# A new order of the pieces in a fused attention and max-out kernel, with a ones product for one more half and whole-tensor packing copies

## The chip, the cores and the metric

The kernel runs on one core of a Trainium2 chip. The metric is the device time of one execution in microseconds (us). Engines named below: PE multiplies matrices into PSUM (PEld loads its weights), DVE and ACT work on vectors and read PSUM, POOL works on SBUF alone and also issues the loads that cast fp32 to bf16, SP issues the stores.

## The reference

Eight batches, eight heads, 576 positions, head size 64, 32 memory slots. An attention over compressed keys and values is followed by a feed-forward layer whose hidden value is the maximum of three products:

```python
a = softmax(phi)                                  # over the 32 slots, per position
k_m = einsum('bhsm,bhsd->bhmd', a, k)             # 32 compressed keys per head
v_m = einsum('bhsm,bhsd->bhmd', a, v)
attn = softmax(q @ k_m.T / 8)                     # over the 32 slots
x = (attn @ v_m), heads side by side              # 4608 x 512
h = max(x @ w1, x @ w2, x @ w3)                   # 4608 x 768
out = h @ w_out                                   # 4608 x 512, fp32
```

## The kernel before

Two identities carry the work. First, the product with v_m is folded into the weights: for each batch, `fold` multiplies v_m into w1 - w3 and w2 - w3, so that the feed-forward reads the attention directly. Second, max(a, b, c) = max(a - c, b - c, 0) + c, so the third product is not formed for every hidden column; w3 times w_out is computed once (`w3_t`, `w3_o`, the tile `w3o`), folded per batch (`wp3`), and added in the last product.

The program is a long list of pieces. Each piece is a word such as `F8@3`: a letter and a number for the kind, and the batch after the @. A sign ! at the end swaps which of ACT and DVE copies the result out of PSUM. The list at the end of the function is written out in full, and every engine runs its share of the pieces in exactly this order; an engine that waits holds up everything behind it on the same engine. The kinds:

- H, L, Y (POOL): loads. H loads a half of k or v of batch 0, L0 phi, L1 k, L2 v, L3 q; Y0 to Y2 load w1 to w3 and Y3 loads w_out. The phi of batch 0 comes from SP. All POOL loads go through one software queue.
- I (POOL): the identity matrix for transposes, and the column of ones in two packed tiles `kvr`.
- r0, r1 (POOL): from batch 2 on, copies k (r0) or v (r1) into `kvr`, where k, v and a one stand side by side for each position.
- E (ACT): exp of phi. B (PE): the compressed keys and values, 72 small products. N (DVE): their division by the sum. K (PE, then DVE or ACT): their transpose. For batches 0 and 1, B, N and K come in two parts, 0 for k and 1 for v.
- Q0, Q1 (DVE): transposes of q. S (PE, then two exps on ACT): scores; it takes two PSUM tiles.
- The second softmax's division, in one of two ways for each batch and half g. The usual one: a (DVE transpose), s (DVE sum), c (DVE reciprocal), m (POOL product), X (DVE transpose back). For the pairs in the set `ONES`: M (PE, a product with a block matrix of ones gives the sums in every row), R (ACT: Ln, then Exp of its negative), X (DVE product).
- D0 to D3 (PE, then a copy to SBUF): fold; D3 makes `wp3`. V (DVE): the differences w1 - w3, w2 - w3, in place.
- F0 to F11 (PE): the feed-forward's first product, one hidden tile each; even ones are copied with relu to `h`, odd ones end in a DVE maximum that writes `hT`. T0 to T4 (PE, ACT copy, SP store): the second product for 128 rows. The last T3 is done in two halves.
- W, O: the one-time product of w3 and w_out. Z: warm-up products that nobody reads.

All PSUM tiles come from one pool of four; a piece that needs a tile waits for the copy out of the tile four places before it. The software DMA queue has eight places for loads in flight, so a load also waits for the landing of the eighth before it. `kvo`, `kvr`, `qT`, `e`, `wp` and others have two buffers.

Lines to follow: `pack` 103, `load_kv` 96, `ones_sum` 326, `ones_rec` 340, `ones_mul` 352, `att_t` 361, `att_mul` 383, `att_back` 393, `fold` 401, `ffn1` 433, `ffn2` 465, the set `ONES` 205, the list 571 to 594.

Of the kernel before, what the change touches and what calls it, by code (L numbers as in the profile page):

```python
# [15 lines left out]
def kernel(  # L16
# [12 lines left out]
    nc = tc.nc  # L29

    B, H, S, D = q.shape
    M = phi.shape[-1]
    P = 128
    NP = H // 2
# [28 lines left out]
    kvos = []  # L63
    for i in range(2):
        kvo = const.tile([P, 3, NP, NC, D], BF16, name=f"kvo{i}")
        kvos.append(kvo)
    kvrs = [
        const.tile([P, NP, NC, 2 * D + 2], BF16, name=f"kvr{i}") for i in range(2)
    ]
# [31 lines left out]
        )  # L101

    def pack(b, i):
        for j in range(NP):
            nc.gpsimd.tensor_copy(  # L105
                out=kvrs[b % 2][:, j, :, D * i : D * (i + 1)], in_=kvos[b % 2][:, i, j]
            )

    def load_q(b):
        qq = inp.tile([P, NP, NC, D], BF16, name="qq")  # L110
# [91 lines left out]
            c = e  # L202

    ln = const.tile([P, S], FP32, name="ln")
    ONES = {(0, 0), (0, 1)}
    st = {}

    def att_exp(b, js=slice(0, NP)):
# [117 lines left out]
    def ones_sum(b, g):  # L326
        s = st[b]
        e2 = s["e2"]
        sm = acc_pool.tile([P, 2, BANK], FP32, name="sm", tag="acc")
        for h in range(2):  # L330
            nc.tensor.matmul(
                sm[:, h, 0:SH],
                lhsT=blkones,
                rhs=e2[:, g, h * SH : (h + 1) * SH],
                start=True,
                stop=True,
            )
        s["sm", g] = sm
# [44 lines left out]
    def att_mul(b, g):  # L383
        s = st[b]
        t = s["t", g]
        nc.gpsimd.tensor_tensor(  # L386
            out=t,
            in0=t,
            in1=s["sm", g].unsqueeze(2).to_broadcast([P, S // HP, R, 2]),
            op=ALU.mult,  # L390
        )
# [146 lines left out]
    def issue(b, n, swap):  # L538

        i = int(n[1:]) if len(n) > 1 else None  # L540
        {
            "I": lambda: [make_identity(nc, ident)]
            + [nc.gpsimd.memset(x[:, :, :, 2 * D : 2 * D + 1], 1.0) for x in kvrs],
            "Y": lambda: load_w(i) if i < 3 else load_wo(),
            "L": lambda: load_ph(b) if i == 0 else load_q(b) if i == 3 else load_kv(b, i - 1),
            "H": lambda: load_kv(b, i % 2, halves[i // 2]),
            "r": lambda: pack(b, i),
            "E": lambda: [att_exp(b, h) for h in (halves if b == 0 else [slice(0, NP)])],
            "B": lambda: att_kv(b, i),
            "N": lambda: att_kv_norm(b, i),  # L550
            "K": lambda: att_kv_t(b, swap, i),
            "Q": lambda: att_q(b, i),
            "S": lambda: att_score(b),
            "a": lambda: att_t(b, i),
            "s": lambda: att_sum(b, i),
            "c": lambda: att_rec(b, i),
            "m": lambda: att_mul(b, i),
            "X": lambda: (ones_mul if (b, i) in ONES else att_back)(b, i),
            "M": lambda: ones_sum(b, i),
            "R": lambda: ones_rec(b, i),  # L560
            "D": lambda: fold(b, i, swap),
            "F": lambda: ffn1(b, i, swap),
            "T": lambda: ffn2(b, i, swap),
            "W": lambda: w3_t(i, swap),
            "O": lambda: w3_o(i, swap),
            "V": lambda: w_diff(i),
            "Z": lambda: warm_up(i),
        }[n[0]]()


    for w in """
        H0@0 H2@0 I@0 L3@0 Y2@0 E@0 Y3@0 Z25@0 B0@0 H3@0 N0@0 Z2@0 K0@0! H1@0 Q1@0 Q0@0 Z9@0
        S@0 Z2@0 M0@0 R0@0 W2@0 M1@0 Y0@0 W0@0 Y1@0 L0@1 R1@0 X1@0 L1@1 X0@0 W1@0! Z7@0 O0@0
        O2@0 O3@0 B1@0 N1@0 O1@0 K1@0 L3@1 D3@0 D1@0 D0@0 F8@0 V0@0 F10@0 F0@0 F6@0! F2@0 L2@1
        D2@0 L1@2 V1@0 D4@0 F4@0 F1@0 F3@0 F11@0 L2@2 F5@0 E@1 F9@0 F7@0 B0@1 N0@1 L0@2 L3@2
        T3@0 K0@1! T1@0 Q0@1 Q1@1 S@1 V2@0 a0@1 T0@0! a1@1 B1@1 s0@1 N1@1 c0@1 K1@1 s1@1 c1@1
        D1@1! D0@1! D2@1 T2@0! m0@1 X0@1 D3@1 m1@1 L1@3 X1@1 F6@1 F2@1! F3@1 F8@1 F10@1 F9@1
        F4@1 E@2 F11@1 r0@2 L2@3 F5@1 F0@1 F7@1 F1@1 r1@2 B@2 T2@1! L3@3 N@2 Q1@2 K@2 L0@3 Q0@2
        T4@1! S@2 a0@2 T3@1 L2@4 D1@2! r0@3 s0@2 D0@2 c0@2 D2@2 a1@2 m0@2 s1@2 c1@2 T0@1! T1@1
        m1@2 X0@2 X1@2 F0@2 L1@4 Q0@3 F6@2 L0@4 F2@2 Q1@3 F4@2 L3@4 F3@2 F5@2 E@3 F1@2 F8@2  # L580
        D3@2 r1@3 B@3 N@3 L1@5 F9@2 F10@2 K@3 F7@2 F11@2 S@3 T0@2! L2@5 a1@3 D0@3 D3@3 T3@2
        r1@4 E@4 s1@3 L0@5 T2@2! a0@3 D1@3! s0@3 c1@3 D2@3 r0@4 B@4 m1@3 c0@3 T1@2 m0@3 X0@3
        Q0@4 X1@3 F10@3 N@4 F0@3 L3@5 F6@3 Q1@4 K@4 L0@6 F4@3 F7@3 F1@3 r0@5 F5@3 F2@3 F3@3
        F8@3 F11@3 F9@3 L2@6 S@4 E@5 r1@5 a0@4 T3@3 a1@4 s1@4 D0@4 D3@4 T4@3! c1@4 s0@4 c0@4
        Q1@5 L1@6 D2@4 m1@4 B@5 D1@4! m0@4 Q0@5 X1@4 X0@4 T1@3 F6@4 N@5 L0@7 L3@6 F2@4 K@5 F3@4
        F8@4 S@5 F7@4 a1@5 r1@6 F10@4 E@6 s1@5 F11@4 a0@5 L2@7 D1@5! D3@5 s0@5 T2@3! F9@4 c0@5
        c1@5 L1@7 F4@4 r0@6 F5@4 F0@4 F1@4 B@6 m0@5 X0@5 E@7 m1@5 N@6 D0@5 L3@7 D2@5 X1@5 Q1@6
        T0@4! Q0@6 r1@7 K@6 F8@5 F2@5 F6@5 F9@5 F0@5 F3@5 r0@7 F4@5 F7@5 S@6 a0@6 F10@5 s0@6
        F11@5 F1@5 F5@5 T0@3! D3@6 c0@6 D0@6 B@7 N@7 T3@5 m0@6 Q1@7 K@7 a1@6 Q0@7 X0@6 s1@6
        T4@5! S@7 T2@4! a0@7 a1@7 s0@7 s1@7 D3@7 c0@7 D2@7 D0@7 T3@4 T2@5! c1@6 c1@7 m1@6 D1@6!  # L590
        D1@7! X1@6 D2@6 m1@7 X1@7 T1@4 F4@6 m0@7 X0@7 T1@5 F8@7 F9@7 F2@6 F3@6 F2@7 F0@6 F6@6
        F5@6 F0@7 F1@6 F7@6 F10@7 F3@7 F6@7 F8@6 F11@7 F1@7 F4@7 F5@7 F9@6 F10@6 F7@7 F11@6
        T0@7! T0@6! T2@7! T1@7 T0@5! T1@6 T2@6! T3@6 T4@7! T3@7
    """.split():
        n, b = w.rstrip("!").split("@")
        issue(int(b), n, w.endswith("!"))
# [30 lines left out]
```

## Time and profile before

| | |
|---|---|
| median of 11 runs | 165.84 us |
| lowest to highest | 165.47 to 166.45 us |
| the profiled execution's own time | 165.97 us |
| its span | 164.2 us |
| TensorE clock granted | 1.00 throughout |
| bytes moved by DMA | 31.77 MB, 68.3% of the engines' time by the software queue |
| stores | 35 of 256 KB and two of 128 KB, 5.5 us from issue to landing for the large ones |

How to read what follows: in the profile's rows, "L443" is line 443 of the kernel; "out<-in" are the program's names; "x48" counts instructions; a timeline row is start, duration (several merged if x is over 1), engine, line and what ended the idle time before it. A busy PE is not a PE at its peak, and idle time of an engine off the chain costs nothing.

### The profile page before, as it was taken

What the parts mean: (1) busy time and instruction counts of PE and PEld (TensorE: products, weight loads), DVE (VectorE), ACT (ScalarE), POOL (GpSimd) and SP (SyncE); (2) the same over time, 40 slices, a digit from 0 to 9 for tenths busy, and PEclk for the clock granted to TensorE, in tenths of its full rate; (3) what the DMA queues carried; (4) which work ended last, traced back from release to release, by engine and by line L of the source; (5) the groups of instructions that cost most, each with busy time, mean ns of one, the idle gap of its engine ahead of it and who ended that gap; (6) DMA issues with size and microseconds to landing.
All of it is one profiled execution on the core that took longest, in us unless ns stands there. A gap on an engine that the chain in (4) does not pass through costs nothing.

```text
span 164.2 us, 4836 instructions
## 1 busy us (share of the span) xinstructions
PE 153.2 (93%) x2061; PEld 85.5 (52%) x2081; DVE 94.0 (57%) x181; ACT 101.3 (62%) x151; POOL 74.0 (45%) x107
## 2 busy tenths in 40 slices
PE   7966898999899999999999999999999999999990
PEld 2432544673367445743684475576534478744450
DVE  6413603698868866685779939968784137900000
ACT  4204735954487188949868979985758976323320
POOL 7931133100399579899757969756207000000000
PEclk9999999999999999999999999999999999999999
DMA  5999999999999999999999999995131330014333
GB/s 152 135 203 208 207 209 214 277 208 208 249 318 237 210 251 319 255 289 208 262 321 284 231 300 258 218 218 124 68 128 64 131 130 0 0 68 178 141 128 130
DMA packets 21974, 31.77 MB, mean 194 GB/s; under 512 B 1216, under 2 KB 16576, under 8 KB 21952
## 3 DMA queue, kind: packets, MB, share of 16 engines
q0 software_dynamic: 16080, 21.43, 68.3%
q1 hardware_dynamic: 5728, 9.90, 17.1%
q8 instruction: 16, 0.26, 0.6%
q10 hardware_dynamic: 144, 0.13, 0.2%
q14 instruction: 6, 0.05, 0.1%
HBM read 39.32 MB, written 9.44 MB: 297 GB/s over the span
## 4 chain that ended last, share of the span: by engine, by line
PE 81%; DMA 9%; issue 2%; POOL 2%; DVE 2%; ACT 1%; ACTq 0%; POOLq 0%
PE po L474 28%; PE acc L443 27%; DMA wo_sb<-in_moe_w_out_dram 9%; PE po L483 8%; PE wps L417 6%; PE kvp L226 4%; PE po L175 3%; PE sc L310 1%; PE po L492 1%; PE kvtp L273 1%; PE po L515 1%; POOL kvo L98 1%; ACT h L153 1%; DVE hT L456 0%; POOL w_sb L118 0%
## 5 line engine op out<-in xcount | busy, mean ns | idle before, releaser
L474 PE MATMUL po<-wo_sb,hT 128*128 128x512 bf16 x193 | 50.3, 380 | 0.9
L443 PE MATMUL acc<-attn,wp 128*128 128x288 bf16 x384 | 49.8, 286 | 0.4 <-DVE wp L159 0.4
L443 PEld LDWEIGHTS <-wp 128*128 128x128 bf16 x384 | 36.8, 98 | 12.5 <-DVE wp L159 0.9
L456 DVE TENSOR_TENSOR hT<-acc,h 128x576 bf16<-128x576 f32 x48 | 34.5, 753 | 13.4 <-PE acc L443 7.3
L155 ACT COPY ot<-po 128x512 f32<-128x512 f32 x35 | 20.7, 592 | 29.4 <-PE po L483 21.9
L105 POOL COPY kvr<-kvo 128x576 bf16<-128x576 bf16 x48 | 29.9, 672 | 10.5 <-DMA kvo<-in_v_dram 5.1
L153 ACT ACTIVATE h<-acc 128x576 bf16<-128x576 f32 x46 | 28.5, 659 | 7.8 <-PE acc L443 6.7
L474 PEld LDWEIGHTS <-hT 128*128 128x128 bf16 x210 | 19.0, 98 | 24.4 <-issue 4.7
L155 ACT CAST wp<-wps 128x1024 bf16<-128x1024 f32 (+1 forms) x31 | 29.5, 1013 | 1.8 <-PE wps L417 1.8
L386 POOL TENSOR_TENSOR t<-t,sm 128x576 bf16<-128x576 bf16 x14 | 16.0, 1153 | 24.8 <-DVE sm L381 24.8
L483 PE MATMUL po<-wp,attn 128*128 128x512 bf16 x62 | 18.4, 379 | 0.0
L142 PE MATMUL po<-warm 128*128 128x512 bf16 x43 | 12.1, 430 | 1.4 <-DVE warm L130 1.2
L288 DVE STREAM_TRANSPOSE qT<-qq 128x576 f32<-128x576 f32 x16 | 11.6, 750 | 1.9 <-DMA qq<-in_q_dram 1.8
L319 ACT ACTIVATE e<-sc 128x576 bf16<-128x576 f32 x16 | 9.6, 652 | 4.9 <-PE sc L310 4.9
L212 ACT ACTIVATE e<-ph 128x1152 bf16<-128x1152 f32 (+1 forms) x9 | 9.5, 1061 | 1.6 <-DMA ph<-in_phi_dram 1.6
L372 DVE TENSOR_REDUCE sm<-t 128x18 f32<-128x576 bf16 x14 | 10.3, 738 | 0.3
L483 PEld LDWEIGHTS <-attn 128*128 128x128 bf16 x62 | 6.1, 98 | 7.2
L394 DVE STREAM_TRANSPOSE attn<-t 128x288 f32<-128x288 f32 x14 | 6.2, 456 | 5.6 <-POOL t L386 5.6
L532 DVE COPY ot<-po 128x256 f32<-128x256 f32 x1 | 0.4, 425 | 15.7 <-PE po L523 15.7
L364 DVE STREAM_TRANSPOSE t<-e 128x288 f32<-128x288 f32 x14 | 6.6, 471 | 4.8 <-ACT e L319 4.6
L98 POOL DMA_DIRECT2D kvo<-in_v_dram x9 | 6.7, 744 | 5.6 <-DMA wo_sb<-in_moe_w_out_dram 3.1
L226 PEld LDWEIGHTS <-e 64*32 64x32 bf16 x720 | 7.1, 90 | 3.7 <-issue 2.8
(59 smaller groups left out, 119.3 us busy)
## 6 DMA issues: line engine op xcount, KB each, us to landing
out_dram<-ot SPq DMA_DIRECT2D x35, 256.0 KB, 5.5
qq<-in_q_dram POOLq DMA_DIRECT2D x8, 576.0 KB, 12.1
ph<-in_phi_dram POOLq DMA_DIRECT2D x7, 576.0 KB, 13.7
kvo<-in_k_dram POOLq DMA_DIRECT2D x7, 576.0 KB, 12.1
kvo<-in_v_dram POOLq DMA_DIRECT2D x7, 576.0 KB, 16.0
w_sb<-in_moe_w_dram POOLq DMA_DIRECT2D x3, 768.0 KB, 19.6
wo_sb<-in_moe_w_out_dram POOLq DMA_DIRECT2D x1, 768.0 KB, 15.2
ph<-in_phi_dram SPq DMA_DIRECT2D x2, 288.0 KB, 2.9
```

The costliest lines, as they stand in the source:

```text
L105: nc.gpsimd.tensor_copy(out=kvrs[b % 2][:, j, :, D * i : D * (i + 1)], in_=kvos[b % 2][:, i, j])
L142: nc.tensor.matmul(po[:, 0:BANK], lhsT=warm[:, 0:P], rhs=warm, start=True, stop=True)
L153: nc.scalar.activation(out=out_, in_=in_, func=AF.Relu)
L155: nc.scalar.copy(out=out_, in_=in_)
L226: nc.tensor.matmul(kvp[M * j : M * (j + 1), a, 0:nd], lhsT=s["e"][r, j, c, :], rhs=kv[r, cols, j, c, :] if b < FULL else kvr[r, j, c, 0:nd ...
L288: nc.vector.transpose(out=s["qT"][:, j].rearrange("p j c r e -> p (j c r e)").bitcast(FP32), in_=loaded[b]["q"][:, j].rearrange("p j c d - ...
L372: nc.vector.tensor_reduce(out=sm, in_=s["t", g].rearrange("p n r e -> p n e r"), op=ALU.add, axis=mybir.AxisListType.X,)
L386: nc.gpsimd.tensor_tensor(out=t, in0=t, in1=s["sm", g].unsqueeze(2).to_broadcast([P, S // HP, R, 2]), op=ALU.mult,)
L443: nc.tensor.matmul(acc[:, h, 0:SH], lhsT=wps[b][:, g, w * DF + ft * P : w * DF + (ft + 1) * P], rhs=attn[:, g, c0 : c0 + SH], start=(g == ...
L456: nc.vector.tensor_tensor(out=hT[:, ft, (b % 2) * S : (b % 2 + 1) * S].rearrange("p (h n) -> p h n", h=2), in0=a, in1=s["h1", ft], op=ALU.max,
L474: nc.tensor.matmul(po, lhsT=hT[:, fc, c0 : c0 + P], rhs=wo_sb[:, fc, :], start=(n == 0), stop=False,)
L483: nc.tensor.matmul(po, lhsT=attn[:, g, c0 : c0 + P], rhs=wp3s[b][:, g, :], start=False, stop=(g == NG - 1),)
```

## The change

Three things change together. `pack` makes one POOL copy for all four pairs of heads (128 x 2304 elements) in place of four copies of 128 x 576. The set `ONES` takes in half 1 of batch 1, so that a1, s1, c1 and m1 of batch 1 go and M1 and R1 of batch 1 come, and X1 of batch 1 becomes a product. And the list is replaced by another order of all pieces, with some swaps of ACT and DVE set differently and 48 warm-up products in place of 45.

```diff
@@ -101,10 +101,9 @@
         )
 
     def pack(b, i):
-        for j in range(NP):
-            nc.gpsimd.tensor_copy(
-                out=kvrs[b % 2][:, j, :, D * i : D * (i + 1)], in_=kvos[b % 2][:, i, j]
-            )
+        nc.gpsimd.tensor_copy(
+            out=kvrs[b % 2][:, :, :, D * i : D * (i + 1)], in_=kvos[b % 2][:, i]
+        )
 
     def load_q(b):
         qq = inp.tile([P, NP, NC, D], BF16, name="qq")
@@ -202,7 +201,7 @@
             c = e
 
     ln = const.tile([P, S], FP32, name="ln")
-    ONES = {(0, 0), (0, 1)}
+    ONES = {(0, 0), (0, 1), (1, 1)}
     st = {}
 
     def att_exp(b, js=slice(0, NP)):
@@ -569,28 +568,28 @@
 
 
     for w in """
-        H0@0 H2@0 I@0 L3@0 Y2@0 E@0 Y3@0 Z25@0 B0@0 H3@0 N0@0 Z2@0 K0@0! H1@0 Q1@0 Q0@0 Z9@0
-        S@0 Z2@0 M0@0 R0@0 W2@0 M1@0 Y0@0 W0@0 Y1@0 L0@1 R1@0 X1@0 L1@1 X0@0 W1@0! Z7@0 O0@0
-        O2@0 O3@0 B1@0 N1@0 O1@0 K1@0 L3@1 D3@0 D1@0 D0@0 F8@0 V0@0 F10@0 F0@0 F6@0! F2@0 L2@1
-        D2@0 L1@2 V1@0 D4@0 F4@0 F1@0 F3@0 F11@0 L2@2 F5@0 E@1 F9@0 F7@0 B0@1 N0@1 L0@2 L3@2
-        T3@0 K0@1! T1@0 Q0@1 Q1@1 S@1 V2@0 a0@1 T0@0! a1@1 B1@1 s0@1 N1@1 c0@1 K1@1 s1@1 c1@1
-        D1@1! D0@1! D2@1 T2@0! m0@1 X0@1 D3@1 m1@1 L1@3 X1@1 F6@1 F2@1! F3@1 F8@1 F10@1 F9@1
-        F4@1 E@2 F11@1 r0@2 L2@3 F5@1 F0@1 F7@1 F1@1 r1@2 B@2 T2@1! L3@3 N@2 Q1@2 K@2 L0@3 Q0@2
-        T4@1! S@2 a0@2 T3@1 L2@4 D1@2! r0@3 s0@2 D0@2 c0@2 D2@2 a1@2 m0@2 s1@2 c1@2 T0@1! T1@1
-        m1@2 X0@2 X1@2 F0@2 L1@4 Q0@3 F6@2 L0@4 F2@2 Q1@3 F4@2 L3@4 F3@2 F5@2 E@3 F1@2 F8@2
-        D3@2 r1@3 B@3 N@3 L1@5 F9@2 F10@2 K@3 F7@2 F11@2 S@3 T0@2! L2@5 a1@3 D0@3 D3@3 T3@2
-        r1@4 E@4 s1@3 L0@5 T2@2! a0@3 D1@3! s0@3 c1@3 D2@3 r0@4 B@4 m1@3 c0@3 T1@2 m0@3 X0@3
-        Q0@4 X1@3 F10@3 N@4 F0@3 L3@5 F6@3 Q1@4 K@4 L0@6 F4@3 F7@3 F1@3 r0@5 F5@3 F2@3 F3@3
-        F8@3 F11@3 F9@3 L2@6 S@4 E@5 r1@5 a0@4 T3@3 a1@4 s1@4 D0@4 D3@4 T4@3! c1@4 s0@4 c0@4
-        Q1@5 L1@6 D2@4 m1@4 B@5 D1@4! m0@4 Q0@5 X1@4 X0@4 T1@3 F6@4 N@5 L0@7 L3@6 F2@4 K@5 F3@4
-        F8@4 S@5 F7@4 a1@5 r1@6 F10@4 E@6 s1@5 F11@4 a0@5 L2@7 D1@5! D3@5 s0@5 T2@3! F9@4 c0@5
-        c1@5 L1@7 F4@4 r0@6 F5@4 F0@4 F1@4 B@6 m0@5 X0@5 E@7 m1@5 N@6 D0@5 L3@7 D2@5 X1@5 Q1@6
-        T0@4! Q0@6 r1@7 K@6 F8@5 F2@5 F6@5 F9@5 F0@5 F3@5 r0@7 F4@5 F7@5 S@6 a0@6 F10@5 s0@6
-        F11@5 F1@5 F5@5 T0@3! D3@6 c0@6 D0@6 B@7 N@7 T3@5 m0@6 Q1@7 K@7 a1@6 Q0@7 X0@6 s1@6
-        T4@5! S@7 T2@4! a0@7 a1@7 s0@7 s1@7 D3@7 c0@7 D2@7 D0@7 T3@4 T2@5! c1@6 c1@7 m1@6 D1@6!
-        D1@7! X1@6 D2@6 m1@7 X1@7 T1@4 F4@6 m0@7 X0@7 T1@5 F8@7 F9@7 F2@6 F3@6 F2@7 F0@6 F6@6
-        F5@6 F0@7 F1@6 F7@6 F10@7 F3@7 F6@7 F8@6 F11@7 F1@7 F4@7 F5@7 F9@6 F10@6 F7@7 F11@6
-        T0@7! T0@6! T2@7! T1@7 T0@5! T1@6 T2@6! T3@6 T4@7! T3@7
+        E@0 I@0 H0@0 H2@0 Z25@0 B0@0 N0@0 Z2@0 K0@0! L3@0 Q1@0 Q0@0 Z9@0 S@0 Z4@0 M1@0 R1@0
+        Y2@0 M0@0 W1@0 X1@0 R0@0 Y3@0 W0@0 W2@0 Z8@0 O0@0 O1@0 O3@0 H3@0 H1@0 B1@0 Y0@0 O2@0
+        Y1@0 X0@0 N1@0 K1@0 D3@0 D1@0 D0@0 V0@0 F10@0 L0@1 F8@0 F6@0 F0@0! F4@0 D2@0 V1@0 D4@0
+        L1@1 F2@0 F1@0 F3@0 F11@0 F5@0 F7@0 E@1 F9@0 B0@1 T1@0 L3@1 L2@1 N0@1 K0@1! Q1@1 L2@2
+        Q0@1 V2@0 T2@0! S@1 a0@1 T3@0 B1@1 L1@2 M1@1 s0@1 c0@1 L0@2 m0@1 R1@1 L3@2 L2@3 N1@1
+        K1@1 D0@1 X0@1 D1@1 D2@1 T0@0! r1@2 X1@1 F10@1 L0@3 F2@1 F4@1 F5@1 F8@1 F0@1 F11@1 E@2
+        L1@3 F1@1 F9@1 L3@3 r0@2 F3@1 F6@1 F7@1 B@2 D3@1 N@2 L2@4 Q1@2 L1@4 T3@1 Q0@2 K@2 L0@4
+        L3@4 T4@1! S@2 T0@1! a0@2 D0@2 s0@2 c0@2 D2@2 r1@3 E@3 D1@2! a1@2 s1@2 c1@2 m0@2 X0@2
+        T1@1 T2@1! m1@2 r0@3 X1@2 F0@2 F8@2 F1@2 F9@2 Q1@3 F10@2 D3@2 L0@5 B@3 L1@5 F4@2 N@3
+        F5@2 r1@4 F6@2 Q0@3 F2@2 r0@4 F11@2 K@3! F3@2 F7@2 D1@3! L2@5 D0@3 T2@2! S@3 E@4 T0@2!
+        a0@3 s0@3 c0@3 T1@2 D3@3 a1@3 s1@3 c1@3 m0@3 X0@3 D2@3 B@4 m1@3 N@4 X1@3 Q0@4 Q1@4 T3@2
+        F8@3 L3@5 K@4 F4@3 L0@6 L1@6 F2@3 F10@3 F9@3 S@4 F5@3 F0@3 a0@4 F11@3 F1@3 L2@6 F6@3
+        E@5 r0@5 F3@3 F7@3 D0@4 a1@4 L3@6 D1@4! s0@4 s1@4 c0@4 r1@5 m0@4 T3@3 T4@3! c1@4 m1@4
+        X0@4 D3@4 D2@4 Q0@5 B@5 T1@3 X1@4 F2@4 N@5 Q1@5 L2@7 K@5 F8@4 F0@4 F3@4 S@5 F9@4 a0@5
+        F6@4 r0@6 F4@4 a1@5 s1@5 F10@4 F1@4 F5@4 E@6 s0@5 L0@7 T2@3! c1@5 F11@4 D0@5 D2@5 F7@4
+        T1@4 c0@5 Q1@6 L1@7 L3@7 D3@5 Q0@6 r1@6 B@6 m1@5 m0@5 X1@5 N@6 D1@5! T3@4 X0@5 F0@5 K@6
+        F8@5 r1@7 E@7 F1@5 S@6 a0@6 F10@5 a1@6 s0@6 s1@6 T0@3! F4@5 F9@5 F6@5 F5@5 F11@5 F2@5
+        F7@5 F3@5 r0@7 c1@6 D0@6 B@7 N@7 Q0@7 Q1@7 D2@6 T1@5 K@7 T4@5! S@7 c0@6 a0@7 a1@7 m1@6
+        s0@7 T2@4! c0@7 s1@7 X1@6 D1@6! m0@7 c1@7 m1@7 m0@6 D3@6 D3@7 X0@7 T0@4! T3@5 D0@7
+        D1@7! D2@7 T2@5! T0@5! X0@6 F10@6 F6@6 F2@6 F4@6 X1@7 F3@6 F5@6 F2@7 F3@7 F8@7 F11@6
+        F7@6 F0@7 F4@7 F8@6 F6@7 F9@7 F5@7 F1@7 F0@6 F10@7 F7@7 F11@7 F9@6 T1@7 F1@6 T0@7!
+        T2@7! T3@6 T0@6! T2@6! T1@6 T4@7! T3@7
     """.split():
         n, b = w.rstrip("!").split("@")
         issue(int(b), n, w.endswith("!"))
```

## The prediction

> **What bounds the kernel now.** I read the page first, then the chain of work that ended last, then busy time in six stretches, then the timelines of PE and POOL where the order changes. Page, part 1:
>
> ```profile
> PE 153.2 (93%) x2061; PEld 85.5 (52%) x2081; DVE 94.0 (57%) x181; ACT 101.3 (62%) x151; POOL 74.0 (45%) x107
> ```
>
> PE is busy 93% of 164.2 us, but 12.1 us of that are warm-up products that nobody reads, so I ask where it does useful work without a break. The chain answers:
>
> ```profile
> 4.99 15.22 DMA wo_sb<-in_moe_w_out_dram
> 20.21 0.14 issue
> 20.34 4.04 PE po L175 x18
> ```
>
> Until 20.21 the end is set by one transfer, the output weights, which stand fifth in the software DMA queue; after it the chain is nearly all PE. Busy time by stretch (columns: length, then PE, PEld, DVE, ACT, POOL busy with counts, clock, DMA share, GB/s):
>
> ```profile
> 20.30:47.00 26.70, 25.01 (x457) 13.04 (x462) 16.63 (x30) 15.09 (x24) 6.90 (x9) 1.00 1.18 234
> 47.00:75.00 28.00, 27.79 (x410) 16.38 (x413) 19.83 (x39) 19.65 (x30) 23.65 (x35) 1.00 1.16 263
> 75.00:105.00 30.00, 29.73 (x515) 17.61 (x518) 21.95 (x46) 25.71 (x37) 23.07 (x32) 1.00 1.16 264
> 105.00:131.00 26.00, 25.74 (x331) 13.63 (x331) 16.89 (x38) 19.84 (x30) 10.52 (x14) 1.00 0.51 131
> ```
>
> From 47 us on PE lacks 0.2 to 0.3 us per stretch; 20.3 to 47 lacks 1.7 us. Start to start in PE's timeline, a piece F takes 0.49 us, T 1.73, T4 1.94, D 0.22, B 0.72, S 0.41; F or T costs 0.09 more before a piece with small tiles (B, S, D), and D 0.11 more before a full-size one. What exceeds these between 20.34 and the last T3 is 2.5 to 2.8 us. So the kernel is a transfer of 20 us, then 140 us of PE work that no order shortens, some 2.7 us of waits, and the last copy and store. The change can move the first term, add PE work, and trade waits.
>
> **The change part by part.** Everything is counted against the profiled execution, 165.97 us (span 164.2), which lies 0.13 above the median of the runs, 165.84.
>
> *The head.* The identity and the two column fills (piece I) move ahead of the first two DMAs on POOL's queue:
>
> ```profile
> 1.25 1.60 POOL L98 DMA_DIRECT2D kvo<-in_k_dram  x2 [0.80 <-POOLq L611]
> 2.84 0.22 POOL masks.py:197 MEMSET ident<- 128x128 bf16 x1
> 3.14 0.29 POOL masks.py:199 TENSOR_SCALAR_AFFINE_SELECT ident<-ident 128x128 bf16<-128x128 bf16 x1
> 3.37 0.41 POOL L543 MEMSET kvr<- 128x36 bf16 x2
> 3.50 0.76 POOL L112 DMA_DIRECT2D qq<-in_q_dram  x1
> ```
>
> Piece I takes 3.50 - 2.84 = 0.66 us. POOL idles 0.80 us before its first DMA, and ACT and SP issue their first instruction at 0.74, so part of the 0.66 can fall into that hole: started at 0.75 it would end at 1.41, and the first DMA is 0.16 late; started at 1.25 it is 0.66 late. The q load and what follows are then issued 0.5 us earlier or as before, which is worth nothing, as they stand in a full queue. The DMA share is near 1 or over it from 2 us on, so a late start should shift the output weights' landing, and all of PE after it. Ends: 0 (the phi loads of SP fill the DMA engines until 3.9 us anyway) and +0.66; I take +0.25, nearer the 0.16, as nothing shown keeps POOL from starting when ACT and SP do. The Trainium skill, DMA: Bandwidth & Descriptors, "Queues, rings and completion order", says that a DMA engine takes packets of its queues in turn; by it the k load would not wait for phi, and the delay would count in full, which speaks against this part. The trace agrees as far as it goes: both queues move data side by side at 42 to 46 us. The sum would be +0.16 to +0.66 by the page and 0 without it.
>
> The other moves before 20.3 us (M1 before M0, the three W evacuations all on DVE, three more warm-ups of 0.22) are hidden by the same transfer: w3 lands at 16.35, and W1, W0, W2 with X1 between them need three copies of 0.69 and a product of 0.76 on DVE from about 17.0, to 19.8, before the landing at 20.2. If the landing came that much earlier, W2 would set the start instead. From 20.34 to 35.5 both orders put the same pieces in the same places under other names (O, O, O, B1, O, K1, D3, D1, D0, twelve F between D2 and D4); the waits there (0.5 before D3, 0.5 before the first F) stay.
>
> *Ones product.* It removes from DVE a 0.47 transpose, a 0.74 sum, a 0.25 reciprocal and a 0.46 transpose, and from POOL a 1.15 product; it adds two PE products (0.25), ACT's Ln and Exp (0.65 + 0.68) and a DVE product of 0.76. The PE piece M1 stands between B1@1 and K1@1, where PE waits:
>
> ```profile
> 42.27 0.75 PE L226 MATMUL kvp<-kvo,e 64*32 64x64 bf16 x72
> 43.44 0.23 PE L273 MATMUL kvtp<-ident,kvn 128*128 128x128 bf16 x1 [0.43 <-DVE kvn L248]
> 43.99 0.84 PE L417 MATMUL wps<-w_sb,kvt 64*32 64x512 bf16 x24 [0.32 <-DVE kvt L159]
> ```
>
> So its 0.25 is free inside the 0.43. ACT: Ln and Exp fill about 43.3 to 44.5, where ACT idled 1.5 us before the fold evacuations at 44.47, so those stay. DVE: kvt to 43.94, X0 to 44.6, D1's evacuation (1.16) to 45.7, the product X1 to 46.4; F10@1 needs it at 46.5. That fits by 0.1; if it slips, F10 pays the slip.
>
> *The POOL chain to B@2.* Before, POOL did this (the next load of q had been issued at 31.11):
>
> ```profile
> 43.64 1.16 POOL L386 TENSOR_TENSOR t<-t,sm 128x576 bf16<-128x576 bf16 x1 [11.79 <-DVE sm L381]
> 46.07 0.80 POOL L98 DMA_DIRECT2D kvo<-in_k_dram  x1
> 46.88 2.48 POOL L105 COPY kvr<-kvo 128x576 bf16<-128x576 bf16 x4
> 49.31 0.74 POOL L98 DMA_DIRECT2D kvo<-in_v_dram  x1
> 50.04 2.48 POOL L105 COPY kvr<-kvo 128x576 bf16<-128x576 bf16 x4
> ```
>
> Now m0@1 is followed by two DMAs, r1@2, three DMAs and r0@2, all in one queue. DVE gives c0@1 at 41.30 + 0.48 + 0.75 + 0.26 and two hand-overs of 0.04 = 42.87 (before, a1 and N1 stood between). POOL: 42.9 + 1.15 + 2 x 0.75 + pack + 3 x 0.75 + pack = 47.8 + 2 packs. A pack of four copies is 2.48, that is 0.61 a copy where one alone takes 0.672; a single copy of the same elements saves the starts of three at most, 0.06 each, so I take 2.42, and r0@2 ends at 52.65. PE: K1@1 at 43.44 as before, D0 D1 D2 to 44.76, T0 to 46.50, twelve F to 52.47. B@2 thus waits 0.2 us, then B@2 and D3@1 end at 53.73, against 53.67 before with D3@1 earlier: this stretch is worth +0.05, the saved change of tile form (0.2) in it. A pack 0.1 us longer costs 0.2. Ends for the pack: 2.28 (the smallest fills take 0.10, which leaves 0.57 of the 0.672 for 576 elements; four times that, the start free), and 2.69 (four times 0.672, nothing saved): -0.2 to +0.6 on this stretch. The row of L386, 1.15 for as many elements but two inputs, would give 4.6 a pack and +4.4; it is another operation and I leave it to the rivals. The Trainium skill, GPSIMD Engine Reference, section 3.1, gives 1.03 cycles an element at 1.2 GHz for simple one-input loops; that is an estimate of 2.0 us for 2304 elements and no wait at B@2. The row of 0.61 us for 576 says 1.06 ns an element, a quarter more, and the sum goes by the row.
>
> The load of q that moved behind m0@1 (31.11 to about 44) is harmless: the transfers ahead of it occupy the queue until 50.4, and S@2 needs it at 57.
>
> *Later stretches.* Gone: K@3 came 1.0 us after B@3 and lost 0.23, it now has five F (2.5 us); S@5 came two F after K@5 and lost 0.14, it now has three; F10@5 after S@6 lost 0.08. That is -0.45. New places of the same kind: S holds two of the four PSUM tiles, and F0@3, F6@4 and T0@3 follow within a piece or two of an S; like F10@5 they may lose about 0.1 each, and K@6 is again two F from its S (0.14 at worst). I take +0.25 of 0 to 0.45. The loads stay ahead of their use: 18 of q, k, v at about 3.5 and 6 of phi at 1.8 us from 40.9 put the last at 115, as before, with S@7 at 121.
>
> Sum: +0.25 + 0.05 - 0.45 + 0.25 = +0.10, so 166.07 on the profiled execution's basis, 165.94 against the median.
>
> **The rivals.** *Slower by the packs:* r0@2 is the last link before B@2 and pays both packs; from 2.6 us a pack (+0.4) it decides, at 2.69 the time is 166.5, and with the head at its full 0.66 it is 166.9. For it: POOL's queue has no slack there. Against: the same bytes, one start. *Slower by the head:* all 0.66 shows, 166.35. For it: the full queue. Against: the 0.80 us hole. *Faster:* phi hides the late start and a pack takes 2.3 or less: 165.94 - 0.25 - 0.2 = 165.5, and 165.2 if none of the new small waits comes. *The ones product does nothing for the time:* DVE is 57% busy and its 1.9 us are off the chain; that is in the forecast already, but if X1 is late by ACT's 1.2 us, F10@1 waits and the time is 167.1.
>
> **How the numbers follow.** A change under 0.2%, 0.33 us, can hardly be told from none. Forecast (within 0.33 of 165.84): 0.38. Packs or a wait on the POOL queue: 0.17; head in full: 0.13; X1 or another wait from the new order: 0.10; faster: 0.22. So 0.22 faster, 0.38 same, 0.40 slower. Range: from the faster case with all its parts, 165.2, to X1's worst case, 167.1, which takes in both slower bounds together.
>
> **What would show it.** Right: the first software DMA at 1.4 to 1.5 us and the output weights landing at 20.4 to 20.5; M1@1 inside the gap before K1@1; one copy of 128x2304 of about 2.4 us; r0@2 ending within 0.3 us of B@2's start; no wait over 0.15 us on PE after 55 us. Wrong: a copy over 2.6 us, the landing after 20.8 or before 20.2, or a wait of PE on X, N or a PSUM tile that I did not place.

## The result and the profile after

The changed kernel takes 167.35 us (median of 12 runs, 167.03 to 167.73) against 165.81 us before (47 runs beside them): a ratio of 1.0087, 95% interval 1.0070 to 1.0103. It is slower by 1.5 us, and the time lies 0.25 us above the upper end of the forecast range. The profiled execution of the changed kernel took 167.03 us (span 165.3), the one of before 165.97 (span 164.2).

The first part of the page, and two of the stretches (length, then PE, PEld, DVE, ACT, POOL busy with counts, clock, DMA share, GB/s), after:

```profile
PE 154.8 (94%) x2065; PEld 86.4 (52%) x2086; DVE 93.6 (57%) x177; ACT 102.8 (62%) x154; POOL 68.4 (41%) x70
```

```profile
20.30:47.00 26.70, 24.59 (x450) 13.08 (x453) 16.81 (x27) 16.71 (x26) 6.93 (x8) 1.00 1.17 237
47.00:75.00 28.00, 26.86 (x411) 16.05 (x413) 17.64 (x34) 20.41 (x30) 19.51 (x17) 1.00 1.16 261
```

The totals hide the loss. In the stretches, PE lacks 2.1 us up to 47 and 1.1 from 47 to 75, where it lacked 1.7 and 0.2 before; the two later stretches are as before. The chain of waits between 43 and 49 us names the place:

```profile
43.59 0.67 PE wps L416 x16
44.26 0.02 issue
44.28 1.23 DVE wp L158
45.51 2.43 DVE attn L353
47.94 0.04 issue
47.98 1.14 PE acc L442 x8
```

Line 353 is `ones_mul`: the product X1@1, the new one of this change. PE ends two products of F10@1 and then waits for it. In order of time, on all engines:

```profile
43.74 0.68 ACT L348 ACTIVATE r<-ln 128x576 f32<-128x576 f32 x1
44.28 1.23 DVE L158 CAST wp<-wps 128x1024 bf16<-128x1024 f32 x1
...
44.44 0.75 POOL L98 DMA_DIRECT2D kvo<-in_v_dram  x1
45.18 2.12 POOL L104 COPY kvr<-kvo 128x2304 bf16<-128x2304 bf16 x1
45.43 2.50 DVE L353 TENSOR_TENSOR attn<-e,r 128x576 bf16<-128x576 bf16 x1
...
46.10 0.41 PE L442 MATMUL acc<-attn,wp 128*128 128x288 bf16 x2
...
47.98 0.40 PE L442 MATMUL acc<-attn,wp 128*128 128x288 bf16 x2 [1.48 <-DVE attn L353]
```

Its inputs are there (`r` is written by 44.42), it starts within 0.3 us of where it was forecast (45.43, forecast 45.7), and it takes 2.50 us where the same line took 0.75 twice in the head of the same execution:

```profile
17.11 0.75 DVE L353 TENSOR_TENSOR attn<-e,r 128x576 bf16<-128x576 bf16 x1
...
18.98 0.75 DVE L353 TENSOR_TENSOR attn<-e,r 128x576 bf16<-128x576 bf16 x1
```

It ends 0.63 us after POOL's copy r1@2.

The ledger, by PE's pieces and the same piece lengths as in the prediction (a wait is what exceeds them):

| us | before | after |
|---|---|---|
| O0 starts | 20.34 | 19.65 |
| waits from there to the last T3 | 2.65 | 4.36 |
| of them F10@1, for X1@1 | 0 | 1.64 |
| behind F4@0: D2@0, for the load of w2 | 0 | 0.40 |
| S@6 | 0 | 0.35 |
| B1@1 and K1@1; M1@1 and K1@1 | 0.97 | 0.74 |
| K@3, S@5, T3@0 | 0.48 | 0 |
| the last T3 starts | 158.54 | 159.61 |

O0's earlier start is chance: w_out landed at 19.5 to 20.5 in all profiled runs, with either head. Of the 0.69 us that it gave, 0.40 were lost again, as PE then came to D2@0 before the load of w2 had landed (30.80). So one wait of 1.64 us, for one DVE instruction, makes the result.

### The profile page after: what moved, and what is told of

Its sections match the earlier page's. It is cut to its first block, busy times and chain, and to the rows that moved or that the text cites. A ratio compares the mean times of both kernels' runs of the same rounds, so it can differ in the third digit from the quotient of the medians.

```text
span 165.3 us, 4801 instructions
## 1 busy us (share of the span) xinstructions
PE 154.8 (94%) x2065; PEld 86.4 (52%) x2086; DVE 93.6 (57%) x177; ACT 102.8 (62%) x154; POOL 68.4 (41%) x70
## 4 chain that ended last, share of the span: by engine, by line
PE 76%; DMA 14%; POOL 4%; DVE 3%; issue 1%; ACT 0%; POOLq 0%; ACTq 0%
PE acc L442 27%; PE po L473 27%; DMA w_sb<-in_moe_w_dram 14%; PE po L482 8%; PE wps L416 5%; PE kvp L225 3%; PE sc L309 2%; POOL kvo L98 2%; DVE attn L353 1%; PE po L491 1%; POOL w_sb L117 1%; PE po L514 1%; PE kvtp L272 1%; DVE wp L158 1%; POOL wo_sb L124 0%
## 5 line engine op out<-in xcount | busy, mean ns | idle before, releaser
L442 PE MATMUL acc<-attn,wp 128*128 128x288 bf16 x384 | 50.7, 286 | 1.8 <-DVE attn L353 1.5
L104 POOL COPY kvr<-kvo 128x2304 bf16<-128x2304 bf16 x12 | 25.4, 2115 | 9.2 <-DMA kvo<-in_k_dram 5.4
L385 POOL TENSOR_TENSOR t<-t,sm 128x576 bf16<-128x576 bf16 x13 | 14.9, 1153 | 34.1 <-DVE sm L380 28.8
L141 PE MATMUL po<-warm 128*128 128x512 bf16 x46 | 13.6, 448 | 1.4 <-DVE warm L129 1.2
L363 DVE STREAM_TRANSPOSE t<-e 128x288 f32<-128x288 f32 x13 | 6.0, 464 | 9.1 <-ACT e L318 9.0
L371 DVE TENSOR_REDUCE sm<-t 128x18 f32<-128x576 bf16 x13 | 9.4, 736 | 0.2
L141 PEld LDWEIGHTS <-warm 128*128 128x128 bf16 x48 | 5.1, 112 | 8.0 <-issue 3.7
L111 POOL DMA_DIRECT2D qq<-in_q_dram x8 | 6.1, 766 | 6.9 <-DVE kvt L158 3.6
L416 PE MATMUL wps<-w_sb,kvt 64*32 64x512 bf16 (+1 forms) x200 | 8.4, 372 | 0.6 <-DMA w_sb<-in_moe_w_dram 0.3
```

Of the source, the lines that this page charges most:

```text
L104: nc.gpsimd.tensor_copy(out=kvrs[b % 2][:, :, :, D * i : D * (i + 1)], in_=kvos[b % 2][:, i])
L141: nc.tensor.matmul(po[:, 0:BANK], lhsT=warm[:, 0:P], rhs=warm, start=True, stop=True)
L385: nc.gpsimd.tensor_tensor(out=t, in0=t, in1=s["sm", g].unsqueeze(2).to_broadcast([P, S // HP, R, 2]), op=ALU.mult,)
L416: nc.tensor.matmul(ps[M * j : M * (j + 1), a, 0 : hi - lo], lhsT=lhs[r, M * j : M * (j + 1)], rhs=rhs[r, j, :], start=(i == 0), stop=(i == ...
L442: nc.tensor.matmul(acc[:, h, 0:SH], lhsT=wps[b][:, g, w * DF + ft * P : w * DF + (ft + 1) * P], rhs=attn[:, g, c0 : c0 + SH], start=(g == ...
```

## The experiments

Ratios are to the kernel before, run on the same chip beside each kernel. Times in the timelines are of one profiled execution each, and the lines shown are chosen from those of all engines. Diffs are shortened: `...` stands for what is left out, and remarks behind # are added.

**e1_split: the packs in four copies again, all else as changed.**

```diff
-        nc.gpsimd.tensor_copy(
-            out=kvrs[b % 2][:, :, :, D * i : D * (i + 1)], in_=kvos[b % 2][:, i]
-        )
+        for j in range(NP):
+            nc.gpsimd.tensor_copy(
+                out=kvrs[b % 2][:, j, :, D * i : D * (i + 1)], in_=kvos[b % 2][:, i, j]
+            )
```

> The changed kernel with each pack as four copies again, order and ones product kept. Theory A (the DVE product X1@1 reads two SBUF tiles and stands still while a POOL copy that reads SBUF runs; in the changed kernel it took 2.50 us in place of 0.75 and ended 0.6 us after the 2.12 us copy r1@2): with copies of 0.67 us it waits for one of them, takes 1.0 to 1.4 us, F10@1 waits 0.3 to 0.7 us in place of 1.6, time 166.1 to 166.6. Theory B (the product is late through the new order or slow through its place, whatever POOL does): 2.5 us again, time 167.3 or, with the longer packs, up to 167.8.

Measured: 166.65 us, ratio 1.0061 (1.0036 to 1.0086). X1@1 took 2.27 us (45.26 to 47.53), and POOL's four copies 3.03 in place of 2.48: the product came in between the third and the fourth copy, which it delayed. F10@1 waited 1.40. Neither theory had this size: the first one let the product wait for one copy, and it waited for three. So the form of the pack is not the cause; a product that starts beside copies has to wait for a gap between them.

**e2_fill: r1@2 as a fill of the same region, 128x2304,** which leaves v of batch 2 out of the result.

```diff
     def pack(b, i):
+        if (b, i) == (2, 1):
+            return nc.gpsimd.memset(kvrs[0][:, :, :, D : 2 * D], 0.5)
```

> The changed kernel with the one copy r1@2 replaced by a fill of the same 128 x 2304 elements, which writes SBUF and reads nothing; v of batch 2 is left out of the computation. Theory A as a matter of the read side: X1@1 takes 0.75 us, F10@1 does not wait (start to start 0.5 us in place of 2.13), time 165.6 to 166.0. Theory A as a matter of any POOL access to SBUF: about 2.5 us as before if the fill is as long, time 167.3. Theory B (order alone): 2.5 us, 167.3.

Measured: 165.87 us, ratio 1.0004 (0.9978 to 1.0029). The timeline of this kernel at the same place:

```profile
45.88 2.05 POOL L105 MEMSET kvr<- 128x2304 bf16 x1
46.13 0.75 DVE L355 TENSOR_TENSOR attn<-e,r 128x576 bf16<-128x576 bf16 x1
```

POOL is as long at work, on the same target, and the product takes 0.75; F10@1 waits for nothing and the whole loss is gone. What counts is that POOL reads SBUF, not that it is busy.

**e3_late: r1@2 moved behind the three loads that followed it.**

```diff
-... T0@0! r1@2 X1@1 F10@1 L0@3 ... L1@3 F1@1 F9@1 L3@3 r0@2 ...
+... T0@0! X1@1 F10@1 L0@3 ... L1@3 F1@1 F9@1 L3@3 r1@2 r0@2 ...
```

> The changed kernel with r1@2 moved behind the three loads L0@3, L1@3, L3@3 on POOL, so that POOL issues loads while X1@1 runs. Theory A: X1@1 0.75 us, F10@1 without a wait; the two copies end at about 52.4 us, so B@2 (due at about 52.1) waits 0.3 us; time 165.7 to 166.1. Theory B: X1@1 still 2.5 us and 167.3 or more.

Measured: 166.96 us, ratio 1.0075 (1.0046 to 1.0104), and the expectation that the product would be free missed. It still took 2.03 us, though POOL only issued loads while it ran, and F10@1 waited 1.2:

```profile
45.09 0.77 POOL L94 DMA_DIRECT2D ph<-in_phi_dram  x1
45.34 2.03 DVE L353 TENSOR_TENSOR attn<-e,r 128x576 bf16<-128x576 bf16 x1
45.83 0.77 POOL L98 DMA_DIRECT2D kvo<-in_k_dram  x1
46.56 0.78 POOL L111 DMA_DIRECT2D qq<-in_q_dram  x1
47.30 2.16 POOL L104 COPY kvr<-kvo 128x2304 bf16<-128x2304 bf16 x1
```

Either the loads held it, or the copy did that stood behind them. This stayed open until e13_probe.

**e4_noones: the ones product of batch 1, half 1 undone.** Its pieces stand as in the old order: a1@1 behind a0@1, and s1@1 c1@1 m1@1 behind K1@1.

```diff
-    ONES = {(0, 0), (0, 1), (1, 1)}
+    ONES = {(0, 0), (0, 1)}
```

> The changed kernel without the ones product for half 1 of batch 1: a1, s1, c1, m1 in the places that they had relative to their neighbours before. No DVE product with two SBUF inputs then stands beside r1@2. Theory A: no 2.5 us instruction; but m1@1 is 1.15 us more on POOL and X1@1 ends at about 46.9, so F10@1 waits about 0.8 us, B@2 0 to 0.3; time 166.3 to 166.8. Theory B (the new order itself loses the time): 167.2 or more.

Measured: 166.39 us, ratio 1.0040 (1.0018 to 1.0063). No DVE product here, but F10@1 waits 0.98 all the same: POOL's division m1@1 stands behind two loads (45.79 to 46.97) and X1@1 behind that. So in this order both ways of the division make F10@1 wait, the ones product 0.66 longer.

**e5_probe: the product by itself.** The kernel before, with seven stretches among its last pieces; in each, one DVE product of X1@1's form (576 a partition, bf16 by fp32) beside something on POOL.

```diff
+        if i in (1, 6):
+            nc.gpsimd.tensor_copy(out=pd, in_=ps_)       # 128x2304
+        elif i == 2: ...                                 # four copies of 128x576
+        elif i in (4, 5): ...                            # three loads, one load
+        nc.vector.tensor_tensor(out=px, in0=pa, in1=src, op=ALU.mult)
```

> The kernel before with seven small pairs put between the last T pieces, where POOL is idle: each time a DVE transpose and then a DVE product of two tiles (576 elements, bf16 and fp32), beside nothing on POOL (0), one copy of 2304 elements (1), four copies of 576 (2), a fill of 2304 (3), three loads (4), one load (5), and again one copy of 2304, but with the product's second input in PSUM (6). Theory A (a POOL instruction that reads SBUF holds up a DVE product with two SBUF inputs until it is over): 0.75 us in 0, 3 and 6; in 1 up to 2 us longer, ending 0.7 us after the copy; in 2 it gets in after one to three copies. The loads tell what a load does: 0.75 if only copies block, 1.3 to 2.0 in 4 if the third late variant was slow through its loads. Theory B (place and order): 0.75 everywhere.

The timeline: POOL idle, beside one copy of 2304, beside four copies:

```profile
145.31 0.71 DVE L580 TENSOR_TENSOR kvo<-kvo,ln 128x576 bf16<-128x576 bf16 x1
...
146.26 2.10 POOL L556 COPY kvo<-kvo 128x2304 bf16<-128x2304 bf16 x1 [18.90 <-DVE kvo L554]
...
146.38 2.59 DVE L580 TENSOR_TENSOR kvo<-kvo,ln 128x576 bf16<-128x576 bf16 x1
...
149.33 1.14 DVE L580 TENSOR_TENSOR kvo<-kvo,ln 128x576 bf16<-128x576 bf16 x1
```

0.71 alone, 2.59 beside the copy: it ends 0.61 after the copy, so it ran when the copy was through. Beside three loads and beside one load it took 0.72 and 0.71, and with its second input in PSUM 0.72 beside a copy of 2304 (copy 175.50 to 177.60, product 175.66 to 176.38). That is the effect in isolation, but for the loads it says the opposite of e3_late. The stretch meant for a fill says nothing, as its product ran beside the last copies.

**e6_pack_alone, e7_ones_alone, e8_head_alone: each part put into the old kernel by itself.** The single copy; the ones product with M1@1 R1@1 behind B1@1; I@0 first in the list.

```diff
-        H0@0 H2@0 I@0 L3@0 Y2@0 E@0 ...
+        I@0 H0@0 H2@0 L3@0 Y2@0 E@0 ...
```

> The kernel before with one copy per pack and nothing else changed. A pack takes 2.1 us in place of 2.48. With the order of before, no product with two SBUF inputs stands beside a pack, so theory A gives 165.5 to 165.9, no change that can be told. If a long copy costs in itself (it holds up other DVE work, or the loads behind it), 166.2 or more.

> The kernel before with the ones product for half 1 of batch 1 alone (M1 and R1 behind B1@1, the packs in four copies, the order otherwise as before). There X1@1 would start at about 46.4 us, with r0@2 on POOL from about 44.8 to 47.3. Theory A: the product waits for a copy, takes 1.3 to 2.3 us, and F6@1 waits 0.5 to 1.7 us: 166.2 to 167.3. Theory B (the new order loses the time, not the product): 165.5 to 165.9.

> The kernel before with the identity and the fills ahead of the first two loads on POOL, nothing else. The prediction's step: +0.16 to +0.66 us, 166.0 to 166.4. The trace of the changed kernel speaks for less: its first load was issued at 1.67 in place of 1.25, but w_out landed at 19.5 in place of 20.2 and w2 at 30.8 in place of 30.6: then 165.4 to 165.9.

Measured: single copy 166.01 us, ratio 1.0005 (0.9980 to 1.0031); ones product 166.71, 1.0033 (1.0005 to 1.0060); head 165.91, 0.9991 (0.9967 to 1.0014). The ones product costs time in the old order too, and in the same way: X1@1 took 1.84 us there, beside the four copies of r0@2 (lengthened to 3.03), and F6@1 waited 0.93. The pack and the head cost and bring nothing by themselves.

**e9_x1first: X1@1 ahead of the evacuation of D1@1, so before the copy begins.**

```diff
-        K1@1 D0@1 X0@1 D1@1 D2@1 T0@0! r1@2 X1@1 F10@1 ...
+        K1@1 D0@1 X0@1 X1@1 D1@1 D2@1 T0@0! r1@2 F10@1 ...
```

> The changed kernel with one piece moved: the product X1@1 stands directly behind the transpose X0@1, ahead of the evacuation of D1@1, so that VectorE comes to it at about 44.45, while POOL issues the load of v (44.44 to 45.18) and before the copy r1@2 begins (45.18). Theory 1, only a POOL instruction that reads and copies in SBUF holds the product, and what held it in the run with the copy moved back was something else: the product takes 0.75 (to 45.2), the evacuation of D1@1 moves by 0.75 to about 46.45, F10@1 waits 0.3 to 0.4 for it in place of 1.64, and the median is 166.0 to 166.3, against 167.35 of the change and 165.87 with the fill. Theory 2, loads that POOL issues into a queue with work outstanding hold the product as well: it is held through the load and then through the copy, to about 47.9, D1@1's evacuation comes behind it, to 49.1, F10@1 waits some 3 us, and the median is about 168.5.

Measured: 170.41 us, ratio 1.0263 (1.0211 to 1.0314), worse than either theory said (five executions took 169.67 to 170.61, one 168.18). The timeline:

```profile
44.89 0.75 POOL L98 DMA_DIRECT2D kvo<-in_v_dram  x1
44.91 3.46 DVE L353 TENSOR_TENSOR attn<-e,r 128x576 bf16<-128x576 bf16 x1 [0.25 <-ACT r L348]
45.62 2.13 POOL L104 COPY kvr<-kvo 128x2304 bf16<-128x2304 bf16 x1
...
48.30 1.21 DVE L158 CAST wp<-wps 128x1024 bf16<-128x1024 f32 x1
```

The product starts 0.71 us ahead of the copy, beside a load, and is held through both. Behind it the evacuation of D1@1 comes 3 us late, and F10@1 waits 3.02 for that, as theory 2 said. What neither theory had is another 1.6 us, and it is PE's clock: between 50.43 and 53.79 fourteen of the F products start 0.24 us after the one before them in place of 0.12. In the stretch from 50.40 to 53.80 the granted clock is 0.50, and 1.00 before it and 0.99 behind it. The page of this run shows it as a 6 among the span's forty slices:

```profile
PEclk9999999999996999999999999999999999999999
```

In no other profiled run is the granted clock under 1.00 between 7 and 161 us; in the changed kernel PE's wait of 1.64 us brought no such drop. The drop begins 0.9 us after the end of PE's wait of 3.02 us; whether that wait brought it was not tested.

**e10_psum: the same order, the second input of X1@1 in PSUM.** ACT's Exp writes 1/sum back into the PSUM tile of the sums.

```diff
         r = work.tile([P, S], FP32, name="r")
+        if b == 1:
+            nc.scalar.activation(out=sm[:, :, 0:SH], in_=ln..., func=AF.Exp, scale=-1.0)
+            return
         nc.scalar.activation(out=r, in_=ln, func=AF.Exp, scale=-1.0)
```

> The changed kernel with the second input of the product X1@1 in PSUM instead of SBUF (ScalarE's Exp writes 1/sum back into the PSUM tile of the sums), and X1@1 moved as in the run with X1@1 first. If what holds the product is two inputs in SBUF beside POOL: it takes 0.75 us whatever POOL does, F10@1 no longer waits for it, but the PSUM tile is held until about 45.2, and D2@1, which takes that tile by the ring of four, waits up to 1.1 us where it waited for nothing; median 166.2 to 166.9. If the lock is by the two engines and not by where the inputs lie, the product is held to about 47.9 and the median is near 168.5.

Measured: 166.41 us, ratio 1.0056 (1.0025 to 1.0087). Beside the same load (44.68 to 45.43) and ahead of the same copy (45.41) the product takes 0.75:

```profile
44.64 0.75 DVE L363 TENSOR_TENSOR attn<-e,sm 128x576 bf16<-128x576 bf16 x1 [0.20 <-ACT sm L349]
45.32 1.22 DVE L158 CAST wp<-wps 128x1024 bf16<-128x1024 f32 x1
```

F10@1 waits for nothing; D2@1, which needs the PSUM tile that is now held longer, waits 0.87. Against e9_x1first, from which it differs in the place of one input alone, 4.0 us are back, 1.6 of them by the clock, which stays at 1.00 here.

**e11_order: the new order alone,** without the ones product (as in e4_noones) and with four copies in each pack (as in e1_split).

> The new order alone: no ones product for the half (1,1), four copies in each pack; a1@1 stands behind a0@1 and s1@1 c1@1 m1@1 behind K1@1, as in the order before. POOL's division m1@1 then ends at about 47.0 and F10@1 waits 1.0 for X1@1, as in the run without the ones product (166.39, 1.0040); the four copies begin behind it and hold up nothing that PE needs. My theory gives 166.3 to 166.5. The rival, that the new order itself is worth what I forecast for its later stretches (0.2 us slower than nothing at most) and only the two other parts cost, gives 165.7 to 166.0.

Measured: 167.92 us, ratio 1.0137 (1.0090 to 1.0184), which neither theory had. F10@1 waits 0.98 for m1@1, as foreseen, but then B@2 waits as well: the packs begin some 1.2 us later, behind m1@1, take 0.37 more each than the single copy, and r0@2 ends after PE wants it (timeline of PE):

```profile
53.71 0.52 PE L226 MATMUL kvp<-kvr,e 64*32 64x129 bf16 x6
54.61 0.75 PE L226 MATMUL kvp<-kvr,e 64*32 64x129 bf16 x66 [0.37 <-POOL kvr L105]
```

By piece lengths B@2 loses 0.81. So the new order is the most costly part when alone, and needs the others: with the single copy it is at 1.0040 (e4_noones), with the ones product at 1.0061 (e1_split), with both at 1.0087. The parts do not add.

**e12_loads: six products beside loads.** The kernel before, and near its end loads on POOL with products of X1@1's form beside them, no copy behind.

```diff
+        for i in range(3):
+            load_w(i)
+        for i in range(3):
+            nc.gpsimd.dma_start(out=kvos[0][:, i]..., in_=by_pair((k, v, q)[i], 7))
+        for x in range(6):
+            nc.vector.tensor_tensor(out=px, in0=pa, in1=ln, op=ALU.mult)
```

> The kernel before with an added stretch behind the last T0@7 group, so that its time as a whole says nothing: one product of the same form as X1@1 (576 a partition, bf16 by fp32, both in SBUF) with POOL idle, then six full loads issued by POOL one behind the other (some 4.6 us, into a queue whose transfers fall behind), and beside them six such products with a transpose behind each. Theory 1 (loads do not hold a product): each product takes 0.71 to 0.76 and the loads 0.75 to 0.8. Theory 2 (loads into a queue with work outstanding do): the first products take 0.7, and from the third or fourth load on, when transfers lag, products take 1.3 to 2 us, ending with the end of a load.

Measured: the three weight loads went out ahead, at 128 us; the other three were issued at 146.53 to 148.76, and three of the products ran beside them. All six took 0.72 to 0.76. Theory 1, as far as it goes: loads alone hold nothing.

**e13_probe: what stands before the loads, behind them, and how many are outstanding.**

```diff
+            (5, tt, lambda: loads(3)),                   # P0
+            (6, copy, lambda: loads(3)),                 # P1
+            (1, lambda: loads(2), copy),                 # P2
+            (1, lambda: loads(3), copy),                 # P3
+            (4, tt, lambda: loads(3), copy),             # P4
+            (5, lambda: [load_w(j) for j in range(3)], lambda: loads(3), copy),   # P5
```

> The kernel before with six added stretches among the last pieces, so that its time as a whole says nothing. In each, VectorE runs two products of X1@1's form (two SBUF inputs, 0.71 alone) beside a sequence on POOL: P0 a product of two SBUF tiles (like m0@1), then three loads, the first VectorE product during the loads; P1 a copy of 2304, then three loads, product during the loads; P2 two loads, then a copy, product during the first load; P3 three loads, then a copy, product during the first load; P4 POOL's product, three loads, a copy, VectorE's product during the loads; P5 six loads with many outstanding, then a copy. Theory a (what stood before the loads keeps the hold for a while): the first product is long, over 1 us, in P0, P1 and P4 and 0.72 in P2 and P3. Theory b (a copy that is next in POOL's order already holds it): long in P2, P3 and P4, in P2 to about the copy's end, 0.72 in P0 and P1. Theory c (loads outstanding): long in P5 alone. If all are 0.72 it stays open.

The timeline of P1, P2, P3 and P4:

```profile
168.47 2.23 POOL L559 DMA_DIRECT2D kvo<-in_k_dram  x3
169.19 0.72 DVE L579 TENSOR_TENSOR kvo<-kvo,ln 128x576 bf16<-128x576 bf16 x1
...
180.32 1.48 POOL L559 DMA_DIRECT2D kvo<-in_k_dram  x2 [9.62 <-DVE kvo L550]
180.37 0.72 DVE L579 TENSOR_TENSOR kvo<-kvo,ln 128x576 bf16<-128x576 bf16 x1
181.40 3.14 DVE L579 TENSOR_TENSOR kvo<-kvo,ln 128x576 bf16<-128x576 bf16 x1
181.79 2.12 POOL L564 COPY kvo<-kvo 128x2304 bf16<-128x2304 bf16 x1
...
189.20 2.23 POOL L559 DMA_DIRECT2D kvo<-in_k_dram  x3 [5.29 <-DVE kvo L550]
189.25 0.71 DVE L579 TENSOR_TENSOR kvo<-kvo,ln 128x576 bf16<-128x576 bf16 x1
190.28 3.88 DVE L579 TENSOR_TENSOR kvo<-kvo,ln 128x576 bf16<-128x576 bf16 x1
191.41 2.14 POOL L564 COPY kvo<-kvo 128x2304 bf16<-128x2304 bf16 x1
...
202.16 2.30 POOL L559 DMA_DIRECT2D kvo<-in_k_dram  x3
202.66 2.45 DVE L579 TENSOR_TENSOR kvo<-kvo,ln 128x576 bf16<-128x576 bf16 x1
204.43 2.64 POOL L564 COPY kvo<-kvo 128x2304 bf16<-128x2304 bf16 x1
```

In P0 and P1, where a POOL product or a copy stands before the loads and nothing behind, all four products took 0.71 to 0.72: theory a falls. With a copy behind the loads a product that starts during a load can be held through the loads and the copy (3.14 in P2, 3.88 in P3, 2.89 in P5), or let in between the last load and the copy, which it then lengthens (P4: 2.45, the copy 2.64). In P5 six loads are outstanding, but a copy stands next as well, so theory c has nothing that b does not explain. What the rows do not fix is from when on the copy counts: the first products of P2 and P3, started beside the first load, 0.05 us after it, passed freely in 0.71 to 0.72.

**e14_fence: POOL's copy kept back until X1@1 is through.** A fill of one column of the copy's target stands between the two on DVE; L3@3 goes behind r0@2 to give POOL the time back.

```diff
     def pack(b, i):
+        if (b, i) == (2, 1):
+            nc.vector.memset(kvrs[0][:, 0, 0, D : D + 1], 0.0)
...
-        ... T0@0! r1@2 X1@1 F10@1 ... L3@3 r0@2 F3@1 ...
+        ... T0@0! X1@1 r1@2 F10@1 ... r0@2 L3@3 F3@1 ...
```

> The changed kernel with X1@1 and r1@2 exchanged in the order and a one-column fill of the pack's target by VectorE between them, so that POOL's copy waits until X1@1 is through; the load L3@3 behind r0@2, to give POOL back the microsecond. If POOL's running copy is what holds X1@1: it starts at about 45.4 to 46.1 and takes 0.75, F10@1 waits at most 0.1, the copy begins about 1.0 later than in the changed kernel, B@2 waits at most 0.2, and the median is 165.7 to 166.2, the time of before. If a copy that only stands next in POOL's order, or the loads ahead of it, hold the product, X1@1 takes 1.3 us or more, F10@1 waits 0.5 to 1.3, and the median is 166.5 to 167.2.

Measured: 165.79 us, ratio 0.9997 (0.9974 to 1.0020). In order of time:

```profile
44.68 0.75 POOL L98 DMA_DIRECT2D kvo<-in_v_dram  x1
45.66 0.75 DVE L355 TENSOR_TENSOR attn<-e,r 128x576 bf16<-128x576 bf16 x1
46.36 0.06 DVE L105 MEMSET kvr<- 128x1 bf16 x1
46.49 2.10 POOL L106 COPY kvr<-kvo 128x2304 bf16<-128x2304 bf16 x1 [1.06 <-DVE kvr L105]
```

A copy that itself waits for a semaphore held nothing here (no load was being issued beside the product either). The product takes 0.75, F10@1 and B@2 wait for nothing, and with this the changed kernel is level with the one before. No version here beats the one before by more than can be told.

## Why the prediction was wrong

It forecast 165.9 us, and put the likeliest loss at the head and the packs. Its steps in turn:

- **X1@1 "a DVE product of 0.76", to 46.4, that "fits by 0.1": the step that failed.** The place, the start and the piece that would pay were right; the duration was not: 2.50 us, and F10@1 paid 1.64. The 0.756 came from the same line in the kernel before, but there both products ran in the head, at 18.77 and 19.44, with POOL idle (from 17.4 to 20.5). The prediction's own sums had POOL's pack run from 45.55 on and the product start at 45.7, and never laid the two side by side. The rival "X1 is late" was priced by ACT's 1.2 us, a lateness of the input, and given 0.10; the lateness was of another kind and 0.4 us more. e2_fill, e10_psum and e14_fence each take the collision away in another way, and the loss goes with it or, in e10_psum, shrinks to a wait for a PSUM tile that the remedy itself brings.
- The Trainium skill, SBUF — State Buffer, "Who interferes with whom", states the rule: a DVE instruction with two inputs in SBUF contends with a GpSimd instruction that reads SBUF, not with one that only writes, and the lock is for the whole instruction. The runs agree: 2.50 beside a copy, 0.75 beside a fill, 0.72 with one input in PSUM, and among four copies the product got in only between two of them (e1_split). The rule, applied to the two rows that the prediction had, would have given an estimate of up to 2.4 + 0.76 us for the product, and the rival its price. One thing does not fit a lock that goes to whoever starts first: in e9_x1first the product started 0.71 us ahead of the copy and was held through it.
- **Head, +0.25: its cost was nothing.** The first load was issued at 1.50 as foreseen (it was 1.25), but w_out did not land later for it: 19.52 to 20.51 in the ten profiled runs with I first, 19.54 to 20.40 in the six without, 20.05 on average in both. So the prediction's other sum for the head, +0.16 to +0.66, did not come either. e8_head_alone bounds it at 0.9967 to 1.0014. The lower end of the step, that phi's transfers hide it, was the right one in size; that phi is why was not tested.
- **M1@1 free: right.** B1@1 and K1@1 lost 0.97 before; with M1@1 between them the two waits are 0.74, and the 0.25 of M1@1 fits in.
- **Pack, 2.42: mis-sized.** A single copy takes 2.12, below the lower end of 2.28. The Trainium skill, GPSIMD Engine Reference, section 3.1, by which I had an estimate of 2.0, was nearer than the row of short copies. It brings nothing alone (e6_pack_alone) and 0.37 a pack where POOL is late: twice that is most of the 0.81 that B@2 waits in e11_order and not in e4_noones.
- **B@2 waits 0.2: it waits for nothing,** in the changed kernel because PE is 1.6 us late itself, in e2_fill, where PE is on time, because the pack is shorter.
- **Later stretches, -0.45 + 0.25: the gains came, the losses were twice as large.** K@3 (0.22) and S@5 (0.14) are gone as foreseen, and so is the 0.08 behind F10@5. Of the new small waits, F0@3 and F6@4 lost 0.08 each, near the 0.1 allowed, and T0@3 nothing; but S@6 lost 0.35 in a way that was not foreseen, so that the net is about nothing in place of -0.20.
- The sum without the one term would have been right: with the product at 0.75 the changed kernel measures 165.79 (e14_fence) and 165.87 (e2_fill), forecast 165.94. That it fits so closely is partly luck: the head's +0.25 and the later stretches' -0.20 both failed to come, and they cancel.

## What to carry to other kernels

A duration from a row holds for what ran beside it. Before moving a DVE operation with two SBUF inputs, lay POOL's timeline of the new order under it; if POOL copies there, or is about to behind some loads, add to its duration the time until that copy ends (a product on POOL was not tried), or let one input stay in PSUM, or make POOL wait. And parts of a change that each do nothing, or little, by themselves can cost together and mend each other; test them in the order in which they will run.

## What the runs showed of the hardware that was not expected

A POOL copy that stands behind loads can hold a DVE product while POOL is still issuing those loads: 3.14, 3.88 and 2.89 us in e13_probe and 3.46 in e9_x1first in place of 0.71 to 0.75, while nine products beside loads with no copy behind took 0.71 to 0.76. A copy that waited for a semaphore did not (e14_fence, with no load being issued). From which instruction ahead the hold begins, and why it let the product in before the copy in P4 and e3_late, is not settled.

The wait at S@6 (0.17 to 0.59 us in every profiled run of the new order, none in the old) is put down by the profile to issue, that is to nothing it shows. It falls between two of the piece's small products, and in e4_noones and e11_order, where PE has four instructions fewer ahead of it, four instructions further on, so it looks tied to a place in PE's stream. What makes it stays open; nothing was tried on it.
